# First transfers, first weights and step order of an attention and FFN kernel rearranged

## The chip, the cores and the metric

The kernel runs on one core of a Trainium2 chip. The metric is the device time in microseconds (us). Of the kernel before, three timed executions are shown, with a median of 879.51 us (879.48 to 880.61); one more execution was taken with the profiler.

## The reference

Eight batches of eight heads, 576 rows of 64 numbers each, are cut into chunks of 64 rows. Each chunk attends to itself alone, and the heads are put side by side into 4608 rows of 512, which go through a two-layer network. q and k are scaled so that the scores spread over a few units.

```python
scores = scale * np.matmul(q_c, k_c.transpose(0, 1, 2, 4, 3))   # per chunk, 64x64
scores = scores - np.max(scores, axis=-1, keepdims=True)
attn = np.exp(scores)
attn = attn / (np.sum(attn, axis=-1, keepdims=True) + 1e-09)
x = np.matmul(attn, v_c)              # -> 4608 x 512
h = x @ w_in                          # 512 x 2048, float64
g = h * (1.0 / (1.0 + np.exp(-1.702 * h)))
return (g @ w_out).astype(np.float32) # 2048 x 512, float64
```

## The kernel before, in words

**Tiles and blocks.** A tile is 128 rows of x; four tiles make a block (`TB`), nine blocks make the output. The inner width of 2048 is cut into 16 columns of 128. Step g of the network is column j = g mod 16 of block g div 16: `h_pe` (two halves, L607 to L609) makes h of the block's 512 rows in one PSUM bank (`hp`, two of them), `g_hi` (L628, L629) applies the activation and rounds, `g_lo` (L633) makes the remainder, and four `o_pe` (L642 to L644, one a tile) add to the four output banks `po0` to `po3`. Every product is made of three matmuls, from a rounded high part and a remainder of each operand. Step 0 is made in two row halves (`h_half`, L611 to L622): the first needs tiles 0 and 1, the second tiles 2 and 3.

**Weights.** Column j of both weight matrices comes in as 8-byte words (`raw_j`: 512 KB of w_in, 512 KB of w_out) and is converted on the core: `scale` and `low` on ScalarE (L172, L176), `high` (two instructions, L181 and L182) and `join` (L188) on VectorE, then `part_h` on ScalarE (L193) and `part_l` on VectorE (L196), all over 1024 columns. The 16 converted columns stay in slots `w0` to `w15` for the whole kernel.

**Attention.** Tiles 0 to 3 are made one by one by `plan_first`, in memory that lies in the still empty slots `w15` to `w8`; the others in pairs by `plan_pair`. A tile goes: load of q and k, load of v (L231); transposes of q and k (`t_pe`, copied out by `t_q` and `t_k`); scores (`s_pe`); `s_max` and `s_sum` on VectorE, `s_exp` on ScalarE, `s_norm` on GpSimd (L308); transposes of the result (`e_pe`, `e_act`); the product with v (`x_pe`); and x rounded (`x_hi`, ScalarE) with its remainder (`x_lo`, VectorE, L342). Pairs from tile 8 on are transposed by VectorE (L425, L491) instead.

**What sets the order.** Nothing is scheduled by a compiler. `Plan.add` takes a step with its engine, a cost, a rank, the events that it needs and makes, and the buffers that it takes and gives. `Plan.emit` runs a clock over these costs: whenever an engine is free, it takes of the steps whose events have come the one of lowest rank whose buffers are free. The events of a step come its cost and a `HANDOVER` later. The order found is written out, and each engine executes its own list in order; the waits on the chip are then real ones. All transfers are one list on SyncE's queue. Where a step's wait on the chip is longer than planned, everything behind it on its engine waits too.

**Ranks around the start.** Tile u of the first four has u - 95 and a little more, so that it goes ahead of every weight step (0.986 j - 3, with `part_h` and `part_l` 3.5 and 2 lower) and of every network step (g and a little). Loads rank by u - 103 (q, k), u - 102.5 (v) and 0.986 j - 8.5 (weights, as two steps, the second needing the first to have landed by the plan). The rows of the pair of tiles 4 and 5 come in at rank -3, its other steps at 0 and above.

Of the kernel before, what the change touches and what calls it, by code (L numbers as in the profile page):

```python
# [21 lines left out]
class Plan:  # L22
# [6 lines left out]
    HANDOVER = {PE: 0.2, ACT: 0.2, DVE: 0.15, POOL: 0.15, DMA: 2.0, None: 0.0}  # L29
# [9 lines left out]
    def emit(self):  # L39
# [13 lines left out]
        table, now, left = None, 0.0, len(self.steps)  # L53
        order = []
        while left:
            for e, heap in ready.items():
                while heap and busy[e] <= now + 1e-9:
# [20 lines left out]
                    post(now + cost + (self.HANDOVER[e] if e == DMA else 0), 0, give)  # L78
# [20 lines left out]
def tile_chunk_attention_ffn(  # L99
# [26 lines left out]
    WARM = 7  # L126
    RANK_1 = (0.0, 7.0)
# [24 lines left out]

    def plan_w(j):
        rank = 0.986 * j - 3.0

        def words():
            word = lambda t, i: w_raw[j].bitcast(t).rearrange("p (n w) -> p n w", w=2)[:, :, i]
            return word(F32, 1), word(I32, 1), word(I32, 0), word(U32, 0)

        def load(part):  # L160
            if part == 0:
                w_raw[j] = const.tile([P, 1024], I64, tag=f"w{j}", name=f"raw_{j}")
                nc.sync.dma_start(
                    w_raw[j][:, :512].rearrange("p (cc f) -> p cc f", cc=NCC),
                    w_in[:, j * P : (j + 1) * P].rearrange("(cc p) f -> p cc f", p=P),
                )
            else:
                nc.sync.dma_start(w_raw[j][:, 512:], w_out[j * P : (j + 1) * P, :])

        def scale():  # L170
            hf, hi, li, lu = words()
            nc.scalar.activation(hf, hf, AF.Copy, scale=2.0**-112)  # L172

        def low():
            hf, hi, li, lu = words()
            nc.scalar.activation(li, lu, AF.Copy, scale=2.0**-29)  # L176

        def high():
            hf, hi, li, lu = words()
            w_tmp[j] = tmp = more.tile([P, 1024], I32, tag="wtmp", name=f"wtmp_{j}")  # L180
# [5 lines left out]
        def join():  # L186
            hf, hi, li, lu = words()
            nc.vector.tensor_tensor(w_tmp[j], w_tmp[j], li, op=ALU.add)  # L188
            w_raw.pop(j)

        def part_h():
            wt[j] = const.tile([P, 2, 1024], F32R, tag=f"w{j}", name=f"w_{j}")
            nc.scalar.activation(wt[j][:, 0, :], w_tmp[j].bitcast(F32), AF.Copy)  # L193

        def part_l():
            nc.vector.tensor_tensor(  # L196
                wt[j][:, 1, :],
                w_tmp.pop(j).bitcast(F32),
                wt[j][:, 0, :].bitcast(F32),
# [5 lines left out]
        e = lambda n: f"{n}_{j}"  # L205
# [35 lines left out]
    def plan_first(u):  # L241
# [3 lines left out]
        k_act = u == 2  # L245
        bc = lambda a: a.unsqueeze(3).broadcast_to([P, NP, 2, CH])

        def load_qk():
# [3 lines left out]
            load_rows(st["raw"], u, (q, k))  # L252

        def load_v():
# [4 lines left out]
            st["et"] = part(2).rearrange("p (n h i) -> p n h i", n=NP, h=2)  # L259
            load_rows(st["v"].unsqueeze(1), u, (v,))  # L260
# [46 lines left out]
        def s_norm():  # L307
            nc.gpsimd.tensor_tensor(st["e"], st["e"], bc(st["r"]), op=ALU.mult)  # L308
# [32 lines left out]
        def x_lo():  # L341
# [3 lines left out]
        plan.add(DMA, 2.0, u - 103, load_qk, make=ev("rows"), take=[slot(0)])  # L345
        plan.add(DMA, 1.0, u - 102.5, load_v, make=ev("v"), take=[slot(1)])
# [4 lines left out]
            PE, 1.2, rank + 0.6, s_pe, need=[ev("tq"), ev("tk"), ev("v")], make=ev("s"),  # L351
# [5 lines left out]
        plan.add(POOL, 1.07, rank + 0.6, s_norm, need=[ev("z")], make=ev("n"))  # L357
# [11 lines left out]
    def plan_pair(u):  # L369
# [114 lines left out]
        def e_dve(c):  # L484
            if c == 0:
                st["et"] = const.tile([P, 2 * NP * 2, CH], F32, tag="et", name=f"eT_{u}")
            for a in range(2):
                for b in range(2):
                    pi = 64 * c + 32 * a
                    po = 64 * c + 32 * b  # L490
                    nc.vector.transpose(  # L491
                        st["et"][po : po + 32, :, 32 * a : 32 * a + 32],
                        st["e"][pi : pi + 32, :, 32 * b : 32 * b + 32],
                    )
# [30 lines left out]
        if pe:  # L525
            for t in range(2):
                plan.add(
                    DMA, 2.0, rank - 3, lambda t=t: load_qk_rows(t), need=[ev("rows0")] if t else [],
# [216 lines left out]
```

## Time and profile before

| what | value |
|---|---|
| median of three timed executions | 879.51 us |
| the profiled execution's own time | 879.57 us |
| its span, first to last instruction | 877.8 us |
| granted TensorE clock, mean of the span | 0.994 |
| TensorE (PE) busy | 860.0 us |
| VectorE (DVE) busy | 389.7 us |
| ScalarE (ACT) busy | 317.7 us |
| GpSimd (POOL) busy | 32.3 us |
| bytes moved by DMA | 55.47 MB |

The profiled execution's time is 0.06 us above the median, and 1.8 us of it lie outside the span. The profile is read from the chain of work that ended last and the stretches in which TensorE was not busy, to the timeline of each engine in the stretch that they point to. The granted clock is a share of full speed: 1.00 is 2.4 GHz, 0.50 is 1.2 GHz.

### The profile page before, as it was taken

How to read it: one execution, taken by the hardware profiler on the slowest of the kernel's cores; microseconds unless marked ns; L12 is line 12 of the kernel's file. 1: busy time of each engine (PE TensorE's matmuls, PEld its weight loads, DVE VectorE, ACT ScalarE, POOL GpSimd, SP SyncE). 2: the span in 40 equal slices, each digit the busy share in tenths (PEclk: the TensorE clock that was granted, in tenths of full speed). 3: DMA queues.
4: the chain of work that ended last, by engine and by line, in shares of the span. 5: the costliest groups of instructions: out<-in, count | busy, mean ns of one | idle time of the engine just before them, and what ended most of it. 6: DMA issues, size and time to landing. Idle time of an engine off the chain costs nothing.

```text
span 877.8 us, 14202 instructions
## 1 busy us (share of the span) xinstructions
PE 860.0 (98%) x5882; PEld 703.2 (80%) x5882; DVE 389.7 (44%) x511; ACT 317.7 (36%) x459; POOL 32.3 (4%) x24
## 2 busy tenths in 40 slices
PE   6699999999999999999999999999999999999998
PEld 5588888888888888888888888888888888888886
DVE  5899985277716253443525171617151411111111
ACT  3999653154323324232423242324232322212221
POOL 1000000001000000000000000000000000000000
PEclk9799999999999999999999999999999999999999
DMA  9996234234442312231222031102010110001001
GB/s 238 315 319 180 48 70 103 36 53 71 82 87 53 59 25 74 47 49 25 67 41 47 16 93 29 26 1 60 13 26 1 25 49 1 0 1 49 1 0 49
DMA packets 194592, 55.47 MB, mean 63 GB/s; under 512 B 179680, under 2 KB 187872, under 8 KB 194528
## 3 DMA queue, kind: packets, MB, share of 16 engines
q1 hardware_dynamic: 194528, 54.57, 27.0%
q8 instruction: 46, 0.75, 0.4%
q14 instruction: 18, 0.15, 0.1%
HBM read 45.09 MB, written 9.44 MB: 62 GB/s over the span
## 4 chain that ended last, share of the span: by engine, by line
PE 94%; SPq 2%; ACT 1%; DMA 1%; DVE 1%; issue 1%; POOL 0%; ACTq 0%; DVEq 0%; POOLq 0%
PE po L642 16%; PE po L643 15%; PE po L644 15%; PE hp L607 15%; PE hp L608 15%; PE hp L609 15%; PE s L443 2%; PE x L504 2%; SPq L231 1%; DMA raw<-in_moe_w_out_dram 1%; ACT raw L172 1%; PE qkTp L410 0%; ACT raw L176 0%; ACT w L193 0%; POOL first_b L308 0%
## 5 line engine op out<-in xcount | busy, mean ns | idle before, releaser
L633 DVE TENSOR_TENSOR g_l<-hp,g_h 128x512 fp32r<-128x512 f32 x144 | 99.2, 689 | 404.5 <-ACT g_h L629 403.9
L642 PE MATMUL po<-w,g_l 128*128 128x512 f32 x576 | 229.5, 398 | 0.1
L629 ACT ACTIVATE g_h<-hp 128x512 fp32r<-128x512 f32 x144 | 86.1, 598 | 395.9 <-PE po L644 395.1
L643 PE MATMUL po<-w,g_h 128*128 128x512 f32 x576 | 226.9, 394 | 0.0
L644 PE MATMUL po<-w,g_h 128*128 128x512 f32 x576 | 224.3, 389 | 0.0
L607 PE MATMUL hp<-x_l,w 128*128 128x512 f32 x572 | 223.6, 391 | 0.0
L609 PE MATMUL hp<-x_h,w 128*128 128x512 f32 x572 | 222.9, 390 | 0.2 <-DVE w L196 0.2
L608 PE MATMUL hp<-x_h,w 128*128 128x512 f32 x572 | 223.1, 390 | 0.0
L642 PEld LDWEIGHTS po<-w,g_l 128*128 128x128 f32 x576 | 108.1, 188 | 25.6 <-DVE g_l L633 0.9
L644 PEld LDWEIGHTS po<-w,g_h 128*128 128x128 f32 x576 | 108.2, 188 | 24.3
L607 PEld LDWEIGHTS hp<-x_l,w 128*128 128x128 f32 x572 | 107.4, 188 | 24.1 <-DVE g_l L633 0.2
L609 PEld LDWEIGHTS hp<-x_h,w 128*128 128x128 f32 x572 | 107.4, 188 | 23.5 <-DVE w L196 0.8
L608 PEld LDWEIGHTS hp<-x_h,w 128*128 128x128 f32 x572 | 107.4, 188 | 22.6
L643 PEld LDWEIGHTS po<-w,g_h 128*128 128x128 f32 x576 | 108.3, 188 | 20.7
L628 ACT ACTIVATE hp<-hp 128x512 f32<-128x512 f32 x144 | 84.3, 586 | 70.9 <-PE hp L609 69.7
L491 DVE STREAM_TRANSPOSE eT<-e 32x512 f32<-32x512 f32 x112 | 78.7, 702 | 20.8 <-PE x L504 17.0
L471 POOL TENSOR_TENSOR e<-e,r 128x1024 f32<-128x1024 f32 x14 | 26.7, 1904 | 604.6 <-DVE r L467 322.1
L425 DVE STREAM_TRANSPOSE qkT<-raw 128x1024 f32<-128x1024 f32 x28 | 34.7, 1240 | 13.2 <-PE s L443 7.3
L516 ACT ACTIVATE x_h<-x 128x512 fp32r<-128x512 f32 x32 | 17.5, 595 | 33.0 <-PE x L504 32.9
L460 ACT ACT_TABLE_LOAD x16 | 20.5, 1283 | 18.9 <-DVE e L457 18.2
L464 DVE TENSOR_REDUCE z<-e 128x16 f32<-128x1024 f32 x16 | 19.5, 1216 | 9.5 <-ACT e L460 8.8
L443 PEld LDWEIGHTS s<-qkT 64*64 64x64 f32 x1024 | 18.2, 135 | 5.7 <-issue 5.7
(64 smaller groups left out, 410.7 us busy)
## 6 DMA issues: line engine op xcount, KB each, us to landing
out_dram<-ob SPq DMA_DIRECT2D x36, 256.0 KB, 2.1
raw<-in_moe_w_in_dram SPq DMA_DIRECT2D x16, 512.0 KB, 7.4
raw<-in_moe_w_out_dram SPq DMA_DIRECT2D x16, 512.0 KB, 8.1
v<-in_v_dram SPq DMA_DIRECT2D x28, 256.0 KB, 3.3
raw<-in_q_dram SPq DMA_DIRECT2D x144, 32.0 KB, 2.0
raw<-in_k_dram SPq DMA_DIRECT2D x144, 32.0 KB, 2.0
raw<-in_q_dram SPq DMA_DIRECT2D x48, 24.0 KB, 1.9
raw<-in_k_dram SPq DMA_DIRECT2D x48, 24.0 KB, 1.8
```

What stands on the lines that cost most here:

```text
L425: nc.vector.transpose(st["tr"][:, i].rearrange("p n (t j) -> p (n t) j", j=32), st["raw"][:, i].rearrange("p n t j -> p (n t) j"),)
L443: nc.tensor.matmul(o, tr[r, 0, n, cols], tr[r, 1, n, cols], start=True, stop=True)
L491: nc.vector.transpose(st["et"][po : po + 32, :, 32 * a : 32 * a + 32], st["e"][pi : pi + 32, :, 32 * b : 32 * b + 32],)
L607: nc.tensor.matmul(hp, wh, xl, start=cc == 0, stop=False)
L608: nc.tensor.matmul(hp, wh, xh, start=False, stop=False)
L609: nc.tensor.matmul(hp, wl, xh, start=False, stop=cc == NCC - 1)
L628: nc.scalar.activation(h_t[g], h_t[g], AF.Gelu_apprx_sigmoid)
L629: nc.scalar.activation(gh, h_t[g], AF.Copy)
L633: nc.vector.tensor_tensor(gl, h_t.pop(g), gh.bitcast(F32), op=ALU.subtract)
L642: nc.tensor.matmul(po, gl[:, c], w[:, 0, :], start=j == 0, stop=False)
L643: nc.tensor.matmul(po, gh[:, c], w[:, 0, :], start=False, stop=False)
L644: nc.tensor.matmul(po, gh[:, c], w[:, 1, :], start=False, stop=j == NF - 1)
```

## The change

The diff does seven things.

- The plan counts a transfer's handover as 2.75 instead of 2.0, takes the table of exp as loaded at the start, and frees the transfer queue in the plan when a transfer has been sent.
- The first loads get new costs and ranks: q and k of a tile 2.4, its v 1.2 (ranks -101.5, -99.7, -99.2, -99.1, and only once its q and k have landed by the plan), a weight column 2.85 as one step. Column 0 of the weights has rank -99.5 and goes into slot `w7` first.
- Column 0 is converted in two parts, the 512 columns of w_in and those of w_out, each by its own six steps; `h` of step 0 needs the first part alone.
- `t_k` of tile 3 moves from DVE to ACT, `s_norm` of tile 0 from POOL to DVE, and `s_pe` of the first tiles no longer needs v.
- The costs of the conversion steps are changed a little.
- In `plan_pair`, the buffer `e` is taken by `s_pe` and no longer by `s_max`, and `e_dve` becomes four steps of two transposes each, where it was two of four.
- In `plan_ffn`, the fourth `o_pe` of a step needs no longer the three others; the buffer `g` is given back by a step without an engine when all four are done.

```diff
-    HANDOVER = {PE: 0.2, ACT: 0.2, DVE: 0.15, POOL: 0.15, DMA: 2.0, None: 0.0}
+    HANDOVER = {PE: 0.2, ACT: 0.2, DVE: 0.15, POOL: 0.15, DMA: 2.75, None: 0.0}
...
-        table, now, left = None, 0.0, len(self.steps)
+        table, now, left = "exp", 0.0, len(self.steps)
...
-                    post(now + cost + (self.HANDOVER[e] if e == DMA else 0), 0, give)
+                    post(now + cost, 0, () if e == DMA else give)
+                    post(now + cost + self.HANDOVER[e], 0, give if e == DMA else ())
...
+    w_in_ready = lambda j: f"w_{j}"
+    w_out_ready = lambda j: f"w_{j}" if j else "wo_0"
+    w_load_rank = lambda j: 0.986 * j - 8.5 if j else -99.5
...
-        plan.add(DMA, 1.6, rank - 5.5, lambda: load(0), need=need, make=e("rawi"), take=[f"w{j}"])
-        plan.add(DMA, 1.6, rank - 5.5, lambda: load(1), need=[e("rawi")], make=e("raw"))
-        plan.add(ACT, 1.1, rank, scale, need=[e("raw")], make=e("wsc"))
-        plan.add(ACT, 1.1, rank, low, need=[e("wsc")], make=e("wlow"))
-        plan.add(DVE, 1.95, rank, high, need=[e("wsc")], make=e("whigh"), take=["tmp"])
-        plan.add(DVE, 1.25, rank, join, need=[e("whigh"), e("wlow")], make=e("wj"))
-        plan.add(ACT, 1.05, rank - 3.5, part_h, need=[e("wj")], make=e("wh"))
-        plan.add(DVE, 1.25, rank - 2, part_l, need=[e("wh")], make=e("w"), give=["tmp"])
+        plan.add(DMA, 2.85, w_load_rank(j), load, need=need, make=f"raw_{j}", take=[f"w{raw_slot}"])
+        parts = [slice(0, 1024)] if j else [slice(0, 512), slice(512, 1024)]
+        n = len(parts)
+        for i, c in enumerate(parts):
+            e = lambda a: f"{a}_{j}_{i}"
+            last = i == n - 1
+            r = rank + 0.1 * i
+            f = lambda step, c=c: lambda: step(c)
+            cost = lambda fixed: fixed + 1.07 / n
+            plan.add(ACT, cost(0.07), r, f(scale), need=[f"raw_{j}"], make=e("wsc"))
+            plan.add(ACT, cost(0.09), r, f(low), need=[e("wsc")], make=e("wlow"))
+            plan.add(
+                DVE, 2 * cost(0) - 0.5 / n + 0.35, r, f(high), need=[e("wsc")], make=e("whigh"), take=[] if i else ["tmp"]
+            )
+            plan.add(DVE, cost(0.16), r, f(join),
+                need=[e("whigh"), e("wlow")] + [f"wj_{j}_{m}" for m in range(i)], make=e("wj"),
+                give=[] if j or not last else [f"w{RAW_0}"])
...
+                ACT, cost(0.0), rank - 3.5, f(part_h), need=[e("wj")], make=e("wh"),
...
+                DVE, cost(0.16), rank - 2, f(part_l), need=[e("wh")], make=both[i],
...
-        k_act = u == 2
+        k_act = u > 1
...
-            nc.gpsimd.tensor_tensor(st["e"], st["e"], bc(st["r"]), op=ALU.mult)
+            eng = nc.gpsimd if u else nc.vector
+            eng.tensor_tensor(st["e"], st["e"], bc(st["r"]), op=ALU.mult)
...
-        plan.add(DMA, 2.0, u - 103, load_qk, make=ev("rows"), take=[slot(0)])
-        plan.add(DMA, 1.0, u - 102.5, load_v, make=ev("v"), take=[slot(1)])
+        plan.add(DMA, 2.4, u - 103, load_qk, make=ev("rows"), take=[slot(0), slot(1)])
+        plan.add(DMA, 1.2, (-101.5, -99.7, -99.2, -99.1)[u], load_v, need=[ev("rows")], make=ev("v"))
...
-            PE, 1.2, rank + 0.6, s_pe, need=[ev("tq"), ev("tk"), ev("v")], make=ev("s"),
+            PE, 1.2, rank + 0.6, s_pe, need=[ev("tq"), ev("tk")], make=ev("s"),
...
-        plan.add(POOL, 1.07, rank + 0.6, s_norm, need=[ev("z")], make=ev("n"))
+        plan.add(POOL if u else DVE, 1.05 if u else 0.72, rank + 0.6, s_norm, need=[ev("z")], make=ev("n"))
...
-            PE, 2.4 if pe else 1.4, rank + 0.6, s_pe, need=need, make=ev("s"), take=["att", "att"], give=["tr"],
+            PE, 2.4 if pe else 1.4, rank + 0.6, s_pe, need=need, make=ev("s"), take=["att", "att", "e"], give=["tr"],
...
-                    DVE, 2.76, rank + 0.6, lambda c=c: e_dve(c), need=[ev("n")] + ([ev("et0")] if c else []),
+                    DVE, 1.38, rank + 0.6, lambda i=i: e_dve(i), need=[ev("n")] + ([ev(f"et{i - 1}")] if i else []),
...
+        plan.add(None, 0, g, None, need=[f"o_{g}_{t}" for t in range(TB)], give=["g"])
...
-                PE, 0.69, g + 2.5, lambda t=t: o_pe(t), need=[ev("gl"), f"w_{j}"]
-                + ([f"o_{g - 1}_{t}"] if j else [])
-                + ([f"o_{g}_{i}" for i in range(t)] if t == TB - 1 else []),
-                make=f"o_{g}_{t}", take=po, give=["g"] if t == TB - 1 else [],
+                PE, 0.69, g + 2.5, lambda t=t: o_pe(t), need=[ev("gl"), w_out_ready(j)]
+                + ([f"o_{g - 1}_{t}"] if j else []),
+                make=f"o_{g}_{t}", take=po,
```

## Rows read from the trace of the kernel before

**Rows 1.** The page: busy time of each engine over the span.

```profile
PE 860.0 (98%) x5882; PEld 703.2 (80%) x5882; DVE 389.7 (44%) x511; ACT 317.7 (36%) x459; POOL 32.3 (4%) x24
```

**Rows 2.** Stretches: us, busy PE, PEld, DVE, ACT, POOL; clock, DMA share, GB/s.

```profile
20.00:30.00 10.00, 2.75 (x40) 2.08 (x40) 7.45 (x12) 6.76 (x8) 2.77 (x2) 0.74 1.06 375
30.00:40.00 10.00, 9.14 (x76) 8.03 (x76) 9.66 (x11) 9.58 (x11) 0.00 (x0) 0.75 1.10 249
40.00:60.00 20.00, 19.87 (x146) 16.15 (x145) 19.49 (x23) 18.73 (x23) 0.00 (x0) 1.00 1.10 336
80.00:100.00 20.00, 19.70 (x206) 15.48 (x205) 18.50 (x21) 15.33 (x20) 0.00 (x0) 1.00 0.21 37
```

**Rows 3.** Timeline of PE and PEld, 31 to 43 us: start, us, what, idle before.

```profile
31.90 0.58 PE L620 MATMUL hp<-x_l,w 128*128 128x256 f32 x1
...
40.67 0.19 PEld L642 LDWEIGHTS po<-w,g_l 128*128 128x128 f32 x1 [0.56 <-DVE g_l L633]
...
42.16 0.39 PE L607 MATMUL hp<-x_l,w 128*128 128x512 f32 x1
...
42.39 0.40 PE L608 MATMUL hp<-x_h,w 128*128 128x512 f32 x1
```

**Rows 4.** Timeline: the first transfers as their users met them.

```profile
5.20 0.65 PE L266 MATMUL qkTp<-ident,first_a 128*128 128x128 f32 x4 [0.15 <-DMA first_a<-in_k_dram]
...
12.43 0.66 PE L266 MATMUL qkTp<-ident,first_a 128*128 128x128 f32 x4 [0.16 <-DMA first_a<-in_k_dram]
...
22.80 1.10 ACT L172 ACTIVATE raw<-raw 128x1024 f32<-128x1024 f32 x1 [3.77 <-DMA raw<-in_moe_w_out_dram]
```

**Rows 5.** Timeline of DVE, 28 to 36 us, whole.

```profile
28.60 0.93 DVE L181 TENSOR_SCALAR wtmp<-raw 128x1024 int32<-128x1024 int32 x1
29.57 1.23 DVE L182 SCALAR_TENSOR_TENSOR wtmp<-raw,wtmp 128x1024 int32<-128x1024 int32 x1
30.71 1.22 DVE L196 TENSOR_TENSOR w<-wtmp,w 128x1024 fp32r<-128x1024 f32 x1
31.84 1.22 DVE L188 CUSTOM_DVE_ANT_0 wtmp<-raw,wtmp 128x2048 uint16<-128x2048 uint16 x1
32.98 0.68 DVE L342 TENSOR_TENSOR x_l<-x,x_h 128x512 fp32r<-128x512 f32 x1
33.58 0.68 DVE L181 TENSOR_SCALAR wtmp<-raw 128x1024 int32<-128x1024 int32 x1
34.30 1.22 DVE L182 SCALAR_TENSOR_TENSOR wtmp<-raw,wtmp 128x1024 int32<-128x1024 int32 x1
```

**Rows 6.** Timeline of ACT around the first activation of the network.

```profile
35.62 1.19 ACT L176 ACTIVATE raw<-raw 128x1024 int32<-128x1024 uint32 x1
36.83 1.28 ACT L628 ACT_TABLE_LOAD   x1
38.13 0.58 ACT L628 ACTIVATE hp<-hp 128x512 f32<-128x512 f32 x1
```

**Rows 7.** Timeline of POOL: `s_norm` of tiles 0 and 3.

```profile
11.45 1.04 POOL L308 TENSOR_TENSOR first_b<-first_b,r 128x512 f32<-128x512 f32 x1 [10.15 <-DVE r L305]
...
27.13 1.85 POOL L308 TENSOR_TENSOR first_b<-first_b,r 128x512 f32<-128x512 f32 x1 [6.21 <-DVE r L305]
```

**Rows 8.** Stretches of one us, columns as in rows 2: the clock.

```profile
24.00:25.00 1.00, 0.00 (x0) 0.00 (x0) 0.97 (x2) 1.00 (x2) 0.00 (x0) 0.93 1.10 382
...
35.00:36.00 1.00, 1.00 (x10) 1.00 (x9) 0.73 (x2) 1.00 (x2) 0.00 (x0) 0.95 0.82 197
```

**Rows 9.** Groups by line: VectorE's transposes of pairs 8 and later.

```profile
L491 DVE STREAM_TRANSPOSE eT<-e 32x512 f32<-32x512 f32 x112 | 78.7, 702 | 20.8 <-PE x L504 17.0 <-POOL e L471 2.1
```

**Rows 10.** Timeline: the last step of weight column 8, its first user.

```profile
79.50 1.22 DVE L196 TENSOR_TENSOR w<-wtmp,w 128x1024 fp32r<-128x1024 f32 x1
...
80.40 0.39 PE L607 MATMUL hp<-x_l,w 128*128 128x512 f32 x1
```

**Rows 11.** Line L168, the loads of w_out: issue to landing.

```profile
DMA to landing us min/median/max: 4.9/8.1/12.1
```

More of the change, by code (lines that the diff above doesn't have):

```diff
@@ L151, in slot_user, with words, load, scale @@
         return divmod(NF - 1 - j, 2)
+    w_in_ready = lambda j: f"w_{j}"
+    w_out_ready = lambda j: f"w_{j}" if j else "wo_0"
+    w_load_rank = lambda j: 0.986 * j - 8.5 if j else -99.5
     def plan_w(j):
         rank = 0.986 * j - 3.0
-        def words():
-            word = lambda t, i: w_raw[j].bitcast(t).rearrange("p (n w) -> p n w", w=2)[:, :, i]
+        both = [w_in_ready(j)] if j else [w_in_ready(j), w_out_ready(j)]
+        raw_slot = j or RAW_0
+        def words(c):
+            word = lambda t, i: w_raw[j].bitcast(t).rearrange("p (n w) -> p n w", w=2)[:, c, i]
             return word(F32, 1), word(I32, 1), word(I32, 0), word(U32, 0)
[L160 to L171, printed above, removed]
+        def load():
+            w_raw[j] = const.tile([P, 1024], I64, tag=f"w{raw_slot}", name=f"raw_{j}")
+            nc.sync.dma_start(
+                w_raw[j][:, :512].rearrange("p (cc f) -> p cc f", cc=NCC),
+                w_in[:, j * P : (j + 1) * P].rearrange("(cc p) f -> p cc f", p=P),
+            )
+            nc.sync.dma_start(w_raw[j][:, 512:], w_out[j * P : (j + 1) * P, :])
+        def scale(c):
+            hf, hi, li, lu = words(c)
             nc.scalar.activation(hf, hf, AF.Copy, scale=2.0**-112)
-        def low():
-            hf, hi, li, lu = words()
+        def low(c):
+            hf, hi, li, lu = words(c)
             nc.scalar.activation(li, lu, AF.Copy, scale=2.0**-29)
-        def high():
-            hf, hi, li, lu = words()
-            w_tmp[j] = tmp = more.tile([P, 1024], I32, tag="wtmp", name=f"wtmp_{j}")
+        def high(c):
+            hf, hi, li, lu = words(c)
+            if j not in w_tmp:
+                w_tmp[j] = more.tile([P, 1024], I32, tag="wtmp", name=f"wtmp_{j}")
+            tmp = w_tmp[j][:, c]
             nc.vector.tensor_scalar(tmp, hi, 3, None, op0=ALU.logical_shift_left)
@@ L184, in high, with join, part_h, part_l @@
             )
[L186 to L195, printed above, removed]
+        def join(c):
+            hf, hi, li, lu = words(c)
+            nc.vector.tensor_tensor(w_tmp[j][:, c], w_tmp[j][:, c], li, op=ALU.add)
+        def part_h(c):
+            if j not in wt:
+                wt[j] = const.tile([P, 2, 1024], F32R, tag=f"w{j}", name=f"w_{j}")
+            nc.scalar.activation(wt[j][:, 0, c], w_tmp[j][:, c].bitcast(F32), AF.Copy)
+        def part_l(c):
             nc.vector.tensor_tensor(
-                wt[j][:, 1, :],
-                w_tmp.pop(j).bitcast(F32),
-                wt[j][:, 0, :].bitcast(F32),
+                wt[j][:, 1, c],
+                w_tmp[j][:, c].bitcast(F32),
+                wt[j][:, 0, c].bitcast(F32),
                 op=ALU.subtract,
@@ L559, in plan_pair @@
         plan.add(
-            PE, 2.4 if pe else 1.4, rank + 0.6, s_pe, need=need, make=ev("s"), take=["att", "att"], give=["tr"],
+            PE, 2.4 if pe else 1.4, rank + 0.6, s_pe, need=need, make=ev("s"), take=["att", "att", "e"], give=["tr"],
         )
-        plan.add(DVE, 2.46, rank + 0.6, s_max, need=[ev("s")], make=ev("m"), take=["e"], give=["att", "att"])
+        plan.add(DVE, 2.46, rank + 0.6, s_max, need=[ev("s")], make=ev("m"), give=["att", "att"])
         plan.add(ACT, 1.05, rank + 0.6, s_exp, need=[ev("m")], make=ev("ex"), table="exp")
```

47 lines of the change are left out of this document (29 added, 18 removed).

## The prediction, made before the change was run

> **What bounds the kernel.** I read the busy times first: TensorE is busy for 860.0 of 877.8 us, no other engine for half of it [rows 1]. Then the stretches [rows 2]: it is busy for 2.75 of the ten us from 20 on and 9.14 of the next ten, at half clock for part of both; after 40 us it is short of full by 0.13 us up to 60 and by 0.30 between 80 and 100. What a change of order can win lies ahead of about 41 us. The PE timeline [rows 3] gives the point to compare at: the first product of step 0 begins at 31.90, the first output product (o0, L642) at 40.67, after a wait for `g_lo` on DVE, and the h of step 2 at 42.16. From there PE simply works off what is left. So the sum asks: when does the changed kernel reach o0 with the same PE work done (four tiles, h of steps 0 and 1, one transposition of the next pair)? The difference is the gain, if nothing stalls later.
>
> In the same stretch DVE and ACT are nearly full too (19.49 and 18.73 of 20 us from 40 to 60 [rows 2]), so the conversions of the weights are as tight as the products.
>
> **The order of the change.** I worked the planner's rule through by hand with the new costs, ranks and handovers up to about 41 us of its clock; from it I take the order alone, and times come from the rows below. The transfers go q0 k0 q1 k1 q2 k2 v0 q3 k3 v1, column 0 of the weights (both parts), v2 v3, columns 1 to 5, then the rows of the next pair. DVE goes, from column 0 on: high (part 0), s_max of tile 3, join (0), high (1), x_lo of tile 1, s_sum of tile 3, part_l (0), join (1), high of column 1, x_lo of tile 2, part_l (1), join of column 1, high of column 2, x_lo of tile 3, part_l of column 1, join of 2, high of 3, high of 4, g_lo of step 0. ACT has, late in this, scale of column 3 ahead of x_hi of tile 3, and scale of columns 4 and 5 ahead of the first activation. PE does the first half of step 0 early, then tile 3, then the second half.
>
> **Transfers.** The k of tiles 0 and 2 came in at 5.20 and 12.43 as second and eighth load [rows 4]: 1.2 us for each 256 KB. A 512 KB half of a weight column takes 524 KB / 375 GB/s = 1.40 us [rows 2]. Before, column 0 is complete after twelve such loads and three halves (the plan put a half of column 1 between): 5.20 + 10 x 1.2 + 3 x 1.4 = 21.4, and its user began at 22.80 [rows 4], 1.4 later. Now it is complete after ten and two halves: 5.20 + 8 x 1.2 + 2 x 1.4 = 17.6, up to 19.0 with that lag; I take the middle, about 18.2. Column 5 comes 2 x 1.2 + 10 x 1.4 = 16.4 later: 34.0 to 35.4, I take 34.7.
>
> **DVE.** Starts follow each other by 1.13 us for a two-input pass over 1024 columns, 0.72 for the shift and 1.14 for the combination behind it, 0.60 for 512 columns [rows 5]. A half `high` is not in the trace: between half of the whole (0.93) and the whole less one 512-column pass (1.86 - 0.60 = 1.26); I take 1.05, near the half, as its passes are the same at half length. The split adds some 4 x 0.1 us to column 0 on DVE, and as much on ACT. The first scale takes a little over half of 1.10 [rows 4], so DVE begins at 18.9. Up to g_lo of step 0 its list holds four half steps of 0.60 (join and part_l, twice) and two of 1.05, s_max of tile 3 (0.72 + 0.60), its s_sum (0.72 and two passes over eight columns, an estimate of 1.1 in all), three x_lo of 0.60, three long passes of 1.13 (join and part_l of column 1, join of 2) and four `high` of 1.86 (columns 1 to 4): 2.4 + 2.1 + 1.3 + 1.1 + 1.8 + 3.4 + 7.4 = 19.5. So g_lo of step 0 can begin at 38.4. Behind x_lo of tile 3 stand two long passes and two `high`, 6.0 us, so that it ends at about 32.5 (before: 33.66 [rows 5]).
>
> **ACT.** The first activation sits behind scale of column 5, which waits for 34.7: 1.15 for scale (1.10 to 1.19 [rows 4, 6]), 1.30 from the table's start to the activation [rows 6], 0.6 for this and 0.6 for the rounding pass behind it, 0.1 of handovers and 0.7 for g_lo [rows 5], 4.45 in all: o0 at about 39.15. DVE's sum gives 38.4 + 0.7, the same. In [rows 6] the activation begins 38.13, 1.32 after the pass ahead of the load ended. The Trainium skill (ScalarE: Activation LUTs, What ACT_TABLE_LOAD costs) counts a drain on top and about 2.66 us for a switch; by that o0 would come 1.3 us later, but no such drain stands in these rows, and the sum goes by them.
>
> **PE.** The second half of step 0 waits for x_lo of tile 3 (32.5). From there to o0 lie twelve half products, twelve whole ones at 0.23 each [rows 3] and eight transposes of 128 columns (an estimate of 1 us): 1.4 + 2.8 + 1 = 5.2 us at full clock, which ends at 37.7 and leaves DVE and ACT to decide. But PE has worked little before that, and [rows 8] shows the clock falling within the 25th us, in a stretch with 2.75 us of work in ten, and coming back only in the 36th, after PE had been at work since before 31.90. At half clock for its first 4 us, which then do 2 us of work, the same list ends at 39.7. Between 39.15 and 39.7 I take 39.5, nearer the row that has the clock low: **1.2 us earlier** than 40.67.
>
> **The rest, at nothing.** The norm of tile 0 on DVE costs 0.69 there and spares 1.04 on POOL [rows 7]; the chain behind it waits for v and for PE anyway; without that cover it would show its 0.7. `t_k` of tile 3 on ACT is hidden in the wait for column 0, up to its 0.6. The smaller transposes are the same 112 of 0.702 us [rows 9], with a place for `g_lo` between; PE waits for none of them after 100 us, so nothing either way (0 to 0.3 us, the idle of [rows 2]). Taking `e` at `s_pe`, and the freed fourth `o_pe`, move PE's steps among work that is there: nothing as long as PE's list is full, 0.69 for each `o_pe` that comes too late. Later weights: column 8 was ready at 80.72 for a product begun at 80.40 [rows 10], so nothing was in hand there. DVE is ahead of before at o0 by 1.2 us and by the `high` of column 4 (1.86), more than PE is; so no new stall.
>
> POOL's norms of tiles 2 and 3 now run beside column 0's conversion. Beside such passes a norm took 1.85 instead of 1.04 [rows 7] and the shift on DVE 0.93 instead of 0.68 [rows 5]: 0.25 us, twice, inside my rounding. The Trainium skill (SBUF — State Buffer, Who interferes with whom) makes it an exclusive lock for a whole instruction; by that a pass of DVE could wait out a norm to its end, which is case B below.
>
> **Sum.** 879.57 of the profiled execution less 1.2 is 878.4; less its 0.06 above the median, **878.3 us**. About 0.2% (1.76 us) is what a measurement of this kernel can tell from no change, so this counts as the same.
>
> **The rivals.** *A: more than that.* The transfers come without the lag (column 5 at 34.0, column 0 at 17.6, so DVE 0.6 us earlier) and the clock stays at its upper level, as PE now has column 0's first products at about 25 us. Then DVE and ACT decide, and o0 comes at 38.5, a gain of 2.2 us: 877.3. For it speaks that the plan's transfer times now agree with [rows 4], against it the long wait of PE ahead of tile 3, and the order itself (x_hi of tile 3 behind scale of column 3) that leaves PE waiting. Chance 0.36. *B: the port.* DVE waits out both norms, of tiles 2 and 3, 2 x 1.04 [rows 7]: o0 at 39.15 + 2.1 = 41.2, 0.5 us later than before, 880.0. Against it: the pass in [rows 5] lost only 0.25. Chance 0.08. *C: slower.* One mechanism: column 5 is sent ahead of the next pair's rows and the first activation waits on ACT behind it. Loads of w_out landed after 8.1 us in the middle, 12.1 at most [rows 11]; if this one takes those 4 us more, it is there at 38.7, o0 at 38.7 + 4.45 = 43.2, **2.5 us later** than before: 882.0. It decides from 36.2 on (40.67 - 4.45). For it: rows of short runs stand right behind it in the queue, and rows take 1.2 us for 256 KB where weights take 1.4 for 512. Against: all ahead of it are weights. Chance 0.14. That the change does nothing to the start can be excluded: column 0 can't land as late as before with three loads fewer ahead of it.
>
> **The numbers.** Forecast 0.42, A 0.36, B 0.08, C 0.14. Forecast and B lie within 0.2%: same 0.50; faster 0.36; slower 0.14. The range takes A down to 1.3 us below its time, 876.0, since neither the half `high` nor the lag is known better, and C up to 881.4, short of its full price.
>
> **What would show it.** Right: column 0's scale begins at 17.6 to 19.0; DVE has hardly a gap from there to g_lo; the first half product of step 0 at about 25; the second at 32 to 33; the first activation directly behind scale of column 5; o0 at 39 to 40; PE full behind it. Wrong: the o0 row later than 41, a gap of PE after 45 us with a weight column as its releaser, or the second half of step 0 well ahead of 32.

## The result, and the profile after

The changed kernel takes 880.80 us, the median of 20 runs (879.80 to 884.14), against 879.59 for the kernel before, also 20 runs: a ratio of the means of 1.0017, 95% interval 1.0009 to 1.0025. It is slower by 0.17% in the mean and by 1.21 us in the median, which is inside the range given and on the other side of the old time than the forecast of 878.3. Its runs also spread more: seven of the 20 lie above 881.5, where none of the kernel before lies above 880.61. The profiled execution took 881.11 and its span is 879.3; TensorE's last product begins at 875.21 where it began at 873.63 before: 1.58 us later.

The page's busy times, to be laid beside [rows 1]:

```profile
PE 862.1 (98%) x5882; PEld 706.7 (80%) x5882; DVE 391.2 (44%) x515; ACT 320.0 (36%) x463; POOL 30.8 (4%) x23
```

The stretches of [rows 2], with the same columns:

```profile
20.00:30.00 10.00, 6.63 (x87) 5.47 (x85) 9.76 (x15) 7.74 (x13) 2.06 (x2) 0.73 1.05 375
30.00:40.00 10.00, 6.43 (x58) 5.82 (x59) 8.71 (x10) 9.30 (x11) 0.00 (x0) 0.59 1.05 291
40.00:60.00 20.00, 18.86 (x143) 15.35 (x142) 17.92 (x19) 17.31 (x20) 0.00 (x0) 1.00 1.11 330
```

The change did what it says: TensorE works 6.63 us of the ten from 20 on, where it worked 2.75. But in the next ten it works 6.43 in place of 9.14, at a lower clock, and from 40 to 60 it now lacks 1.1 us. TensorE's waits past 31 us, from its timeline, are three; they answer to [rows 3]:

```profile
34.70 0.58 PE L651 MATMUL hp<-x_l,w 128*128 128x256 f32 x1 [2.94 <-DVE x_l L373]
42.78 0.50 PE L673 MATMUL po<-w,g_l 128*128 128x512 f32 x1 [1.14 <-DVE g_l L664]
63.83 0.50 PE L673 MATMUL po<-w,g_l 128*128 128x512 f32 x1 [1.20 <-DVE g_l L664]
```

The second is the first output product, o0: 42.78, where it was 40.67, with the same work done. The third has no counterpart in the trace of before. Both wait for a `g_lo`, so the next views are those of the engines that make it. DVE, around the first:

```profile
37.55 1.23 DVE L190 SCALAR_TENSOR_TENSOR wtmp<-raw,wtmp 128x1024 int32<-128x1024 int32 x1
40.30 0.69 DVE L451 COPY qkT<-qkTp 128x512 f32<-128x512 f32 x1 [1.52 <-PE qkTp L441]
40.91 1.22 DVE L196 CUSTOM_DVE_ANT_0 wtmp<-raw,wtmp 128x2048 uint16<-128x2048 uint16 x1
42.04 0.69 DVE L664 TENSOR_TENSOR g_l<-hp,g_h 128x512 fp32r<-128x512 f32 x1
```

and ACT, around the first gelu and around the first exponential of a pair ([rows 6] answers to the first three lines):

```profile
36.82 1.19 ACT L178 ACTIVATE raw<-raw 128x1024 f32<-128x1024 f32 x1 [0.64 <-DMA raw<-in_moe_w_out_dram]
38.03 1.28 ACT L659 ACT_TABLE_LOAD   x1
39.33 0.58 ACT L659 ACTIVATE hp<-hp 128x512 f32<-128x512 f32 x1
39.94 0.60 ACT L660 ACTIVATE g_h<-hp 128x512 fp32r<-128x512 f32 x1
...
56.75 1.16 ACT L178 ACTIVATE raw<-raw 128x1024 f32<-128x1024 f32 x1 [1.64 <-DMA raw<-in_moe_w_out_dram]
57.94 1.28 ACT L491 ACT_TABLE_LOAD   x1
59.23 1.06 ACT L491 ACTIVATE e<-e 128x1024 f32<-128x1024 f32 x1
60.31 1.28 ACT L659 ACT_TABLE_LOAD   x1
61.60 0.58 ACT L659 ACTIVATE hp<-hp 128x512 f32<-128x512 f32 x1
```

An engine takes its instructions strictly in the order in which they were written. At 36.82 ACT has waited 0.64 us for a transfer (scale of column 5), with the gelu of step 0 behind it in its queue. At 40.30 DVE has idled 1.52 us for a transposition (`t_k` of the next pair), with `g_lo` behind it and a join between, although `g_h` was done at 40.54. At 56.75 ACT has waited 1.64 us for column 9, with the exponential, two table loads and the gelu of step 3 behind it.

DVE's earlier passes, and the norms of GpSimd that ran beside them (answering to [rows 5, 7]):

```profile
19.88 1.41 DVE L190 SCALAR_TENSOR_TENSOR wtmp<-raw,wtmp 128x512 int32<-128x512 int32 x1
...
23.58 0.69 DVE L190 SCALAR_TENSOR_TENSOR wtmp<-raw,wtmp 128x512 int32<-128x512 int32 x1
...
26.45 1.53 DVE L196 CUSTOM_DVE_ANT_0 wtmp<-raw,wtmp 128x1024 uint16<-128x1024 uint16 x1
...
33.97 0.68 DVE L373 TENSOR_TENSOR x_l<-x,x_h 128x512 fp32r<-128x512 f32 x1
```

```profile
19.68 1.07 POOL L339 TENSOR_TENSOR first_b<-first_b,r 128x512 f32<-128x512 f32 x1 [0.54 <-DVE r L335]
26.12 1.32 POOL L339 TENSOR_TENSOR first_b<-first_b,r 128x512 f32<-128x512 f32 x1 [5.38 <-DVE r L335]
```

The same pass takes 1.41 on the first half of column 0, beside a norm, and 0.69 on the second half, alone. The clock, in stretches of one us of TensorE (busy time, clock, DMA share, GB/s), falls and comes back here ([rows 8]):

```profile
24.00:25.00 1.00, 0.07 (x4) 0.81 1.12 424
25.00:26.00 1.00, 1.00 (x33) 0.50 0.97 355
37.00:38.00 1.00, 1.00 (x5) 0.50 0.71 171
38.00:39.00 1.00, 1.00 (x6) 0.86 1.04 365
```

So there are four suspects: the order (steps on the path queued behind steps that wait), the transfers' order, the split of column 0 with its passes beside GpSimd, and the half clock (1.2 of 2.4 GHz), which lasts from 24.6 to 38.3 where it lasted from 24.9 to 35.1. Twelve kernels tell them apart, in the order in which they ran. Each was timed beside the kernel before, whose median was then 879.59 to 879.76. A profile holds one execution, and the start differs between executions: the second half of step 0, at 34.70 here, begins at 33.60, 34.15 and 33.45 in runs 1 to 3, whose list is the same up to there.

### The profile page after: what moved, and what is told of

The parts are those of the page before. It is cut to its first block, busy times and chain, and to the rows that moved or that the text cites. A ratio compares the mean times of both kernels' runs of the same rounds, so it can differ in the third digit from the quotient of the medians.

```text
span 879.3 us, 14187 instructions
## 1 busy us (share of the span) xinstructions
PE 862.1 (98%) x5882; PEld 706.7 (80%) x5882; DVE 391.2 (44%) x515; ACT 320.0 (36%) x463; POOL 30.8 (4%) x23
## 4 chain that ended last, share of the span: by engine, by line
PE 92%; SPq 3%; DMA 2%; ACT 1%; DVE 0%; issue 0%; DVEq 0%; ACTq 0%
PE hp L638 15%; PE po L674 15%; PE po L673 15%; PE po L675 15%; PE hp L639 14%; PE hp L640 14%; DMA raw<-in_moe_w_out_dram 2%; PE x L535 2%; PE s L474 2%; SPq L261 1%; SPq L170 1%; SPq L174 1%; PE eTp L509 0%; PE qkTp L441 0%; ACT raw L178 0%
## 5 line engine op out<-in xcount | busy, mean ns | idle before, releaser
L673 PE MATMUL po<-w,g_l 128*128 128x512 f32 x576 | 226.1, 392 | 2.3 <-DVE g_l L664 2.3
L638 PE MATMUL hp<-x_l,w 128*128 128x512 f32 x572 | 226.9, 397 | 0.0
L550 DVE TENSOR_TENSOR x_l<-x,x_h 128x512 fp32r<-128x512 f32 x32 | 21.2, 686 | 28.6 <-ACT x_h L547 28.6
```

What stands on the lines that cost most here:

```text
L638: nc.tensor.matmul(hp, wh, xl, start=cc == 0, stop=False)
L673: nc.tensor.matmul(po, gl[:, c], w[:, 0, :], start=j == 0, stop=False)
```

## The experiments

**1. `g_lo` of step 0 ahead of `t_k` and the join.** The order that the planner wrote is edited by hand before it is issued; runs 1 to 3 differ in the list of moves alone:

```diff
+        for step, behind in [('gl_0', 'gh_0')]:
+            s = order.pop(names.index(step))
...
+            k = names.index(behind) + 1
+            order.insert(k, s)
```

> The changed kernel with g_lo of step 0 (L664 there) put on VectorE directly behind g_hi of step 0, ahead of t_k of the pair and the join of column 3. Theory of the order (in-order engines, g_lo queued behind t_k and the join): g_lo starts at 40.6 us in place of 42.04, TensorE meets it at the end of the second product row of step 1 (41.6), so its wait of 1.14 us ahead of the first output product is gone and that product starts at 41.6 in place of 42.78; by itself 1.1 us less, 879.7 in place of 880.8. Rival, the next wait is a transfer's: ScalarE's exponential of the first pair (59.23) stands behind the scale of a weight column whose w_out half lands at 56.7 whatever TensorE does, so TensorE's wait of 1.20 at 62 us grows to about 2.3 and the time stays at 880.5 to 880.9. Rival, the order is not the cause (the port or the clock is): first output product within 0.3 of 42.78.

Measured: 880.77, ratio 1.0016 (1.0007 to 1.0025). TensorE's waits past 40 us:

```profile
44.25 0.50 PE L647 MATMUL hp<-x_h,w 128*128 128x512 f32 x1 [0.75 <-DVE w L211]
63.48 0.50 PE L680 MATMUL po<-w,g_l 128*128 128x512 f32 x1 [1.20 <-DVE g_l L671]
```

o0 comes at 41.39, its wait is gone, and nothing is won. The wait moved: the join that was pushed back now holds a weight column for step 2 by 0.75, and behind column 9 the next one stands as it was. The theory's 879.7 was wrong. The first rival had the total right, but for another reason than it gave: the wait at 63 did not grow.

**2. The exponential ahead of the wait for column 9.**

```diff
-        for step, behind in [('gl_0', 'gh_0')]:
+        for step, behind in [('wsc_9_0', 'gh_3')]:
```

> The changed kernel with the scale of column 9 (the one that waits 1.64 us for its w_out half at 56.75) moved on ScalarE behind g_hi of step 3, so that the first pair's exponential (L491) and the gelu of step 3 no longer stand behind that transfer. Theory of the order: exponential ends by 57.6 in place of 60.3, gelu of step 3 starts at about 58.9 in place of 61.60, g_lo at 60.4 in place of 63.10, TensorE's wait of 1.20 at 62 us is gone, the first output product stays at 42.8; 1.2 us less, 879.6. Rival, weights become the limit a step later (the column's scale and join 3 us later): a wait of TensorE on a weight column of about the same size between 65 and 80, 880.8.

Measured: 879.34, 0.9997 (0.9988 to 1.0006), 1.5 under the changed kernel. The exponential begins at 55.92 in place of 59.23, TensorE's only wait past 40 us is that at 42.87, and none took the place of the one at 63:

```profile
55.92 1.06 ACT L498 ACTIVATE e<-e 128x1024 f32<-128x1024 f32 x1
```

```profile
42.87 0.50 PE L680 MATMUL po<-w,g_l 128*128 128x512 f32 x1 [1.13 <-DVE g_l L671]
```

The first theory holds for this wait.

**3. Both.**

```diff
-        for step, behind in [('gl_0', 'gh_0')]:
+        for step, behind in [('gl_0', 'gh_0'), ('wsc_9_0', 'gh_3')]:
```

> Both moves together. Theory of the order, with the second wait bound by the transfer: the two add up, 2.3 us less than the changed kernel, 878.5, which is 1.0 under the kernel before; first output product 41.6, no wait of over 0.5 us on TensorE between 45 and 66. Rival, order is not the cause: 880.5 or more. Rival, the transfers of the weights bound this stretch (16 columns of 1 MB one behind the other): a wait on a weight column shows between 60 and 80, and the time is 879.5 to 880.5.

Measured: 879.30, 0.9998 (0.9989 to 1.0006): no better than run 2 alone, and not the theory's 878.5. o0 is at 41.27, and h of step 2 waits 0.74 for a weight column at 44.14. Moving single steps by hand mends one wait and leaves the steps around it where they were.

**4. The late parts alone,** on the kernel before: the parts of the diff from `e_dve` on, without the planner's load costs:

```diff
-        def e_dve(c):
+        def e_dve(i):
...
-            PE, 2.4 if pe else 1.4, rank + 0.6, s_pe, need=need, make=ev("s"), take=["att", "att"], give=["tr"],
+            PE, 2.4 if pe else 1.4, rank + 0.6, s_pe, need=need, make=ev("s"), take=["att", "att", "e"], give=["tr"],
...
+        plan.add(None, 0, g, None, need=[f"o_{g}_{t}" for t in range(TB)], give=["g"])
...
```

> The kernel before with only the parts that act past the first 40 us: the transposes on VectorE in four steps, the buffer of the scores' exponentials taken at the score products, and output products of a step in any order of their tiles. Theory: the changed kernel is 3.1 us behind at 100 to 140 us and 1.5 behind at the end, so these parts give back 1.6 us: 878.0 against 879.6. Rival: they are worth nothing as predicted (0 to 0.3) and the lag shrinks by something else (the clock, or waits that both orders share): 879.3 to 879.7. Rival: without the rest they disturb the order between 45 and 100 us, where weights still arrive: slower than 879.8.

Measured: 877.78, 0.9979 (0.9970 to 0.9988). These parts are worth 1.85 us, more than the theory had, where the prediction had nothing. So the rest of the change costs about 3 us, not 1.2, if the two parts add up.

**5. The clock held, on that kernel.** Products of the unit matrix into an unused tile:

```diff
+                    if make in self.hold:
+                        order.append(self.hold[make])
...
+    def hold(n):
+        ps = ps_o.tile([P, P], F32, tag="po0", name="hold")
+        for _ in range(n):
+            nc.tensor.matmul(ps, ident, ident, start=True, stop=True)
+    plan.hold = {"ep_2": lambda: hold(30), "xp_2": lambda: hold(18), "ep_3": lambda: hold(8)}
```

> The kernel before with the late parts (the last run of the first four), and 128x128 products of the unit matrix into an unused tile behind the transposes of tile 2 (30), the value products of tile 2 (18) and the transposes of tile 3 (8), in stretches where TensorE waits there (3.90, 1.93 and 0.81 us), so that TensorE isn't idle ahead of step 0. Theory, the half clock of 25 to 35 us costs time: granted clock 0.9 or more from 25 to 38, both halves of step 0 in 2.8 us in place of 4.6, first product of step 1 at about 34.7 in place of 36.2; 0.8 to 1.5 us less than without them (877.8), 876.3 to 877.0. Rival, what follows is held by ScalarE (table load, columns' scales) and VectorE, not by TensorE: steps 0 and 1 earlier, but the first output product within 0.4 us and 877.6 to 878.0. Rival, the added products are late themselves at half clock: slower than 878.0.

Measured: 882.02, 1.0030 (1.0018 to 1.0041). The third case in its time, though not for its reason, as the clock is at its upper level throughout. It is a mis-sized experiment: each such product is two passes of 0.114 us, so the first thirty took 6.86 us in a wait of 3.9. It says nothing of the clock's worth; run 11 repeats it with fewer.

**6. The clock held, on run 3:**

```diff
+    plan.hold = {"ep_2": lambda: hold(8), "xp_1": lambda: hold(11), "xp_3": lambda: hold(18)}
```

> The changed kernel with both moves of the third run, and such products of the unit matrix behind the transposes of tile 2 (8), the value products of tile 1 (11) and of tile 3 (18), where TensorE waits 1.49, 1.75 and 3.15 us. Theory, the half clock until 38.8 us costs 1.0 us between the end of step 0 (36.2 in both kernels' orders) and the pair's transposes (38.74 against 37.76): granted clock 0.9 or more from 33 to 40, second half of step 0 in 1.4 us in place of 2.75, and 1.0 to 1.5 us less than 879.3, 877.8 to 878.3. Rival, the next wait takes it (a weight column: 0.74 at 44.14 in the run without): 879.0 to 879.4.

Measured: 879.27, 0.9995 (0.9986 to 1.0004), the same as run 3. From 30 to 38 us and from 38 to 42 the clock is whole (it was 0.65 and 0.86 in run 3):

```profile
30.00:38.00 8.00, 7.87 (x82) 1.00 1.09 285
38.00:42.00 4.00, 3.17 (x16) 1.00 1.15 313
```

and TensorE waits here:

```profile
38.67 0.63 PE L450 MATMUL qkTp<-ident,rows 128*128 128x128 f32 x4 [0.53 <-DMA rows<-in_k_dram]
41.01 0.50 PE L682 MATMUL po<-w,g_l 128*128 128x512 f32 x1 [0.31 <-DVE g_l L673]
43.88 0.50 PE L649 MATMUL hp<-x_h,w 128*128 128x512 f32 x1 [0.75 <-DVE w L213]
```

The first two waits are new and stand where the slow products were; the third, which the rival named, stood in run 3 (0.74). The half clock is covered: a faster TensorE meets the pair's rows and `g_lo` sooner.

**7. The first transfers in their ranks of before,** the rest of the change kept:

```diff
-    w_load_rank = lambda j: 0.986 * j - 8.5 if j else -99.5
+    w_load_rank = lambda j: 0.986 * j - 8.5
...
-        plan.add(DMA, 1.2, (-101.5, -99.7, -99.2, -99.1)[u], load_v, need=[ev("rows")], make=ev("v"))
+        plan.add(DMA, 1.2, u - 102.5, load_v, need=[ev("rows")], make=ev("v"))
```

> The changed kernel with the ranks of its first transfers as before (column 0 behind the rows of all four tiles, v of a tile right behind its rows); the planner orders all else anew, and in what it writes the scale of column 5 stays ahead of the first gelu, and t_k and the join of column 3 ahead of g_lo of step 0. Theory of the order: both waits stay (first output product later than 42, a wait of over 1 us at 60 to 64), 880.3 to 881.3. Rival, the order of the transfers is what cost the time: 879.5 or less, first output product before 42.

Measured: 880.53, 1.0015 (1.0006 to 1.0024): not told apart from the changed kernel. The wait at o0 stays (43.29, 1.12). The one at 62 is gone from the profiled execution, unlike expected, for ACT's wait for column 9 shrank to 0.48. The order of the first transfers isn't what costs the 3 us.

**8. Column 0 in one part:**

```diff
-        parts = [slice(0, 1024)] if j else [slice(0, 512), slice(512, 1024)]
+        parts = [slice(0, 1024)]
```

with one event for both halves of the column.

> The changed kernel with column 0 converted in one part as before; in the order that the planner then writes the scale of column 5 stands behind the first two gelus, g_lo of step 0 behind t_k but ahead of the join of column 3, and the first exponential of a pair behind the gelu of step 4. Theory of the order: the wait of 1.2 us at 62 is gone or under 0.4, the first output product comes at 41.5 to 42.2; 879.0 to 879.8 although step 0 starts later. Rival, the split buys time by itself (step 0's first half runs under the wait for tile 3): without it step 0 ends 1 to 2 us later and the time is 881.0 to 882.5.

Measured: 878.10, 0.9986 (0.9977 to 0.9995), 2.7 under the changed kernel and below the theory's range; o0 is at 40.85. ACT's list around the first gelu is

```profile
35.52 1.28 ACT L659 ACT_TABLE_LOAD   x1
36.82 0.58 ACT L659 ACTIVATE hp<-hp 128x512 f32<-128x512 f32 x1
```

with no scale of column 5 ahead of it. This run doesn't tell whether the split costs by its passes or by the order that the planner writes around them; the next run does.

**9. One number of the planner,** the split kept:

```diff
-        plan.add(DMA, 2.85, w_load_rank(j), load, need=need, make=f"raw_{j}", take=[f"w{raw_slot}"])
+        plan.add(DMA, 3.15, w_load_rank(j), load, need=need, make=f"raw_{j}", take=[f"w{raw_slot}"])
```

> The changed kernel with one number of the planner raised: a column's load 3.15 us in place of 2.85 (on the chip column 5 lands at 36.8 and column 9 at 56.7, the planner has them at 34.25 and 52.85). Column 0 stays in two parts; the planner now writes the scale of column 5 behind the first two gelus, g_lo of step 0 ahead of t_k and the join, and the scale of column 9 behind the gelu of step 3. Theory (the loads' planned landings are too early, so steps that wait for them are put ahead of the path): first gelu at 38.5 or earlier, first output product at 40.6 to 41.5, no wait over 0.5 us on TensorE at 62; 878.0 to 879.0. Rival (the split itself costs, by its passes on VectorE and ScalarE): 879.2 or more, as with the moves by hand (879.3).

Measured: 877.57, 0.9977 (0.9968 to 0.9986): 3.2 us under the changed kernel and 2.0 under the kernel before. ACT:

```profile
36.20 1.28 ACT L659 ACT_TABLE_LOAD   x1
37.50 0.58 ACT L659 ACTIVATE hp<-hp 128x512 f32<-128x512 f32 x1
...
51.16 1.16 ACT L178 ACTIVATE raw<-raw 128x1024 f32<-128x1024 f32 x1 [0.80 <-DMA raw<-in_moe_w_out_dram]
```

TensorE's last wait of over 0.15 us, and o0, which follows the transposes without one:

```profile
33.58 0.58 PE L651 MATMUL hp<-x_l,w 128*128 128x256 f32 x1 [3.36 <-DVE x_l L373]
...
39.81 1.03 PE L441 MATMUL qkTp<-ident,rows 128*128 128x128 f32 x8
40.60 0.48 PE L673 MATMUL po<-w,g_l 128*128 128x512 f32 x1
```

VectorE's list from x_lo of tile 3 to `g_lo` is the one that the prediction had worked out, with `high` of column 4 ahead of `g_lo`; the first and the last of it are

```profile
32.84 0.68 DVE L373 TENSOR_TENSOR x_l<-x,x_h 128x512 fp32r<-128x512 f32 x1
...
39.44 0.68 DVE L664 TENSOR_TENSOR g_l<-hp,g_h 128x512 fp32r<-128x512 f32 x1
```

ACT still waits for a transfer at 51.16, but the gelu behind it, at 53.24, comes in time for TensorE, and no exponential stands there. The split isn't the cause: it is here whole, and so are the smaller parts of the change that were not tried by themselves. The planner's list was built on a column 5 that lands at 34.25 (by its own clock: begun at 28.65, 2.85 for the load, 2.75 of handover) and met one at 36.8. Only this one cost was tried: that the planned landing must be near the real one, and not just different, isn't shown, and run 8 brought 2.7 us with the cost as it was. Against run 3, o0 comes 0.67 sooner and the wait of 0.74 behind it is gone: 1.4 of the 1.7 us between the two.

**10. The norms on VectorE,** on top of run 9:

```diff
-            eng = nc.gpsimd if u else nc.vector
-            eng.tensor_tensor(st["e"], st["e"], bc(st["r"]), op=ALU.mult)
+            nc.vector.tensor_tensor(st["e"], st["e"], bc(st["r"]), op=ALU.mult)
```

> The same, with the norms of all four first tiles on VectorE, so that no pass of VectorE runs beside one of GpSimd there (three norms of 0.72 more on VectorE). Theory of the port (in the changed kernel two passes beside a norm took 1.41 and 1.53 us in place of 0.69 and 0.68): the passes of L190 and L196 on half columns are all back at 0.7, VectorE's list to x_lo of tile 3 gets 3 x 0.72 - 1.57 = 0.6 us longer at most, and TensorE's waits for transposed weights behind a norm get shorter: x_lo of tile 3 within 0.7 us, the time within 0.4 of the run before this one. Rival, the waits beside a norm are not GpSimd's doing: the passes stay at 1.4, x_lo of tile 3 is 2 us later and the time 0.5 to 1.5 more.

Measured: 877.73, 0.9978 (0.9969 to 0.9987), no different from run 9. The passes that took 1.41 and 1.53 in run 9, and x_lo of tile 3 (32.84 there), in this run:

```profile
18.89 0.69 DVE L190 SCALAR_TENSOR_TENSOR wtmp<-raw,wtmp 128x512 int32<-128x512 int32 x1
...
25.94 0.69 DVE L196 CUSTOM_DVE_ANT_0 wtmp<-raw,wtmp 128x1024 uint16<-128x1024 uint16 x1
...
32.69 0.68 DVE L372 TENSOR_TENSOR x_l<-x,x_h 128x512 fp32r<-128x512 f32 x1
```

The lengthening is GpSimd's doing, and what it costs is about what the norms cost DVE itself. It is not a matter of two inputs: in run 1 the shift over the first half of column 0, a pass with one input that takes 0.42 alone, took 1.18 beside a norm and ended 0.29 behind it, first DVE, then GpSimd:

```profile
18.23 1.18 DVE L196 TENSOR_SCALAR wtmp<-raw 128x512 int32<-128x512 int32 x1 [0.29 <-ACT raw L185]
```

```profile
18.07 1.05 POOL L346 TENSOR_TENSOR first_b<-first_b,r 128x512 f32<-128x512 f32 x1 [0.54 <-DVE r L342]
```

**11. The clock held, on run 4,** run 5 at half the length or less:

```diff
-    plan.hold = {"ep_2": lambda: hold(30), "xp_2": lambda: hold(18), "ep_3": lambda: hold(8)}
+    plan.hold = {"ep_2": lambda: hold(15), "xp_2": lambda: hold(8), "ep_3": lambda: hold(3)}
```

> The kernel before with the late parts and half as many unit products as in the fifth run (15, 8 and 3, each of them two passes of 0.11 us), which fit into TensorE's waits (3.4, 1.8 and 0.7 us). Theory of the clock: granted clock 0.9 or more from 25 to 38, step 0 starts within 0.4 us of 31.6 and ends at about 34.4 in place of 36.2; 0.5 to 1.5 us less than 877.8. Rival (as in the changed kernel with the clock held: 0.0): what follows waits for transfers and VectorE; 877.5 to 878.1.

Measured: 877.47, 0.9977 (0.9968 to 0.9986), against 877.78 without: just under the rival's range of 877.5 to 878.1 and above the theory's 876.3 to 877.3, so nearer the rival. The clock is 1.00 from 25 to 38 us, where run 4 had 0.61, and the time turns up as waits:

```profile
32.20 0.39 PE L624 MATMUL hp<-x_h,w 128*128 128x256 f32 x1 [0.48 <-DVE w L198]
33.93 0.39 PE L622 MATMUL hp<-x_l,w 128*128 128x256 f32 x1 [0.28 <-DVE x_l L344]
36.93 0.50 PE L611 MATMUL hp<-x_h,w 128*128 128x512 f32 x1 [0.83 <-DVE w L198]
```

**12. The order of the output products alone,** on the kernel before:

```diff
+        plan.add(None, 0, g, None, need=[f"o_{g}_{t}" for t in range(TB)], give=["g"])
...
-                + ([f"o_{g - 1}_{t}"] if j else [])
-                + ([f"o_{g}_{i}" for i in range(t)] if t == TB - 1 else []),
-                make=f"o_{g}_{t}", take=po, give=["g"] if t == TB - 1 else [],
+                + ([f"o_{g - 1}_{t}"] if j else []),
+                make=f"o_{g}_{t}", take=po,
```

> The kernel before with one of the late parts alone: the output products of a step in any order of their tiles (the last tile's no longer behind the others). Theory: this part carries the gain of the late parts (0.9 of 2.1 us of the profile's difference lies ahead of 134 us, where there are no transposes on VectorE): 877.8 to 878.6. Rival, the transposes in four steps and the buffer taken earlier carry it: 879.3 to 879.8 here.

Measured: 877.53, 0.9978 (0.9969 to 0.9987). It carries all of run 4; the smaller transposes and the earlier `e` add nothing that can be measured, as predicted. Between points at which TensorE has begun the same products of each kind, it takes 649.92 us in the kernel before (99.54 to 749.46) and 648.58 here (98.86 to 747.44), though both show it busy for 20.00 of 20 us in every stretch between. A part of that is seen in the products with v of one pair, first before, then here:

```profile
140.97 1.48 PE L504 MATMUL x<-eT,v 64*64 64x64 f32 x64
```

```profile
141.48 1.16 PE L504 MATMUL x<-eT,v 64*64 64x64 f32 x64
```

## Why the prediction was wrong

- **The frame.** Where TensorE stands at o0 is the right point for the early part: 2.1 us later. What follows did not simply work off: a new gap of TensorE at 62 us (its last product before it begins at 62.24, the next at 63.83, 1.36 beyond the 0.23 of an ordinary step) adds 1.4, and the late parts give back what run 12 gains behind o0, 1.7: 2.1 + 1.4 - 1.7 = 1.8, near the 1.58 of the profile. "What a change of order can win lies ahead of about 41 us" was read from busy shares and is wrong by this 1.7.
- **What o0 is made of.** Forecast 39.5. x_lo of tile 3 ended 2.15 later than worked out ("DVE"), and from there TensorE needed 7.0 us to the end of its products (34.65 to 41.64), as many as lie between 32.5 and 39.5; then it waited 1.14 for `g_lo` ("The order of the change"). Together 42.79; measured 42.78.
- **"The order of the change" is the first step that failed.** For DVE it ended "high of 3, high of 4, g_lo of step 0". In the list that ran, `t_k` of the next pair and the join of column 3 stand there and `high` of column 4 comes later. The sum counted each step's duration and none's wait, and `t_k` waits for TensorE. `g_lo` began 1.5 us behind `g_h`'s end: 42.04 against 40.54. Run 9 has the forecast's list for DVE there, and its o0 is at 40.60: with the order as worked out, 1.1 of the forecast gain of 1.2 were still missing.
- **"Transfers".** Column 0 came as worked out. Column 5 was put at 34.7 and ACT stood waiting for it until 36.82. That is past rival C's point of 36.2, and by C's own sum o0 would come at 36.82 + 4.45 = 41.3. But TensorE's own products ended at 41.64, so at o0 this wait decided nothing. C's mechanism, which had a chance of 0.14, did come about one table load later, at column 9.
- **"ACT".** Its sum held: from scale of column 5 to `g_h`'s end lie 3.72 us (36.82 to 40.54), 3.65 by its terms. The switch took 1.32 from the end of the pass ahead to the activation, as in the rows.
- **"DVE" is the second step that failed: its term for the norms was mis-sized.** It began column 0 at 19.45 in place of 18.9, and x_lo of tile 3 ended at 34.65 in place of 32.5. Of the 2.15 us the later start is 0.55; it belongs to this execution, as run 9 began at 18.32. The two passes beside a norm, 0.72 and 0.85 longer than alone, are 1.57. The term "0.25 us, twice" was a third of that.
- **The norms, and rival B.** That term was read from a shift that began 0.38 us ahead of its norm's end (28.60 against 28.98 [rows 5, 7]), while here the passes began 0.87 and 0.99 ahead of it. All three ended 0.54 to 0.55 us behind their norm's end. That a shift has one input and these passes two makes no such difference, as run 1 shows (below run 10). So rival B's mechanism, a wait for the norm's end, is what happened, at 1.57 in place of its 2.1 us. The Trainium skill (SBUF — State Buffer, Who interferes with whom) calls it an exclusive lock for a whole instruction; the trace agrees for these passes. Not every pass is held: x_lo of tile 2, which began at 28.00 in the kernel before, inside the norm of 27.13, took its usual 0.68. By run 10 the total is the same when DVE makes the norms itself.
- **"PE".** The half clock lasted until 38.3 as TensorE waited 2.94 us for x_lo of tile 3. The step took the right row for it, but in runs 6 and 11 it wasn't a term of the time: held at its upper level, the kernels of runs 3 and 4 take the same time within 0.3 us.
- **"So no new stall."** It rested on DVE's lead at o0, which didn't come about, and it didn't look at ACT's queue at the next table load, where column 9 did at 56.75 what column 5 had done at 36.82. Run 2 puts it at 1.5 us.
- **"The rest, at nothing".** Right for the transposes and for `e`, wrong for the output products, 2.0 us (run 12). Freed of their order they were priced as a loss for each one that comes late; a gain wasn't considered. At the same products begun, run 12 is 0.3 us ahead of the kernel before at o0 (40.40 in place of 40.67), 0.7 at 100 us, 1.2 at 150 and 2.0 from 750 on. A wait of 0.30 that the kernel before has at 88.31 is gone; the rest is products that follow each other a little faster. Why the freed order does that stays open.

Runs 4, 9 and 12 agree to 0.25 us. So the early part, with its order mended, brings nothing over run 12. The traces show that x_lo of tile 3, for which TensorE waits, ends no sooner: at 33.52 in run 9, 33.66 in the kernel before and 33.42 in run 12. DVE, busy for 17.3 of the 20 us from 20 on in run 12, is busy for 19.7 of them in run 9, with the norms' 1.57 among them: the 5.6 us by which it begins column 0 sooner (18.32 against 23.93) are gone when x_lo of tile 3 comes. What would have to move was not tried and stays open.

## What to carry to other kernels

When a planner writes a fixed order for in-order engines, its error costs time where a step that waits for a transfer is put just ahead of one on the path: here 0.3 us on one load's cost was worth 3.2 us, while the same waits mended by hand brought 1.5. It is worth trying to give loads the time at which their users meet them on the chip, and after a change to look in each engine's queue for the first instruction that waits and what stands behind it. Price a moved step by its wait as well as its duration, a pass beside another engine by how early in that engine's instruction it begins, and a freed constraint as a possible gain. And a busy share of 20.00 in 20 us doesn't mean that nothing can be won there: run 12 won 1.3 us in such stretches.

## What was not expected of the hardware

- A pass of VectorE over 512 columns beside a norm on GpSimd took 1.41 and 1.53 us, 0.69 and 0.68 alone, and ended 0.54 us behind the norm both times. It goes the other way too: the norm of 1.32 (1.04 alone) began at 26.12 while DVE was in a pass from 25.90 to 26.54, and ended 0.90 behind that pass; the norm of 1.85 in [rows 7] ended 0.90 behind a join (26.90 to 28.08).
- One DMA issue held SyncE for 4.44 us (those ahead of it 0.4 to 1.3, later ones up to 3.4), in the line below (its columns are those of the timelines), and the transfer rate, 364 GB/s at 16 us, fell to 97 at 19 before it recovered. Whether this made column 5 late isn't shown; run 9 has one of 4.18 at the same place:

```profile
14.24 4.44 SPq L170 DMA_DIRECT2D raw<-in_moe_w_in_dram  x1
```

- Products of no use, put into TensorE's waits, kept the granted clock at 1.00 from 25 to 38 us (run 11); without them its mean there was 0.61 (run 4), falling to half towards the end of a wait of 3.90 us of TensorE (up to 25.54).
